# A fused adaLN block with sliding attention and MLP: V of the last blocks four at a time, Q and K of the last tokens two head groups at a time, and a new order of the work

## The chip, the cores and the metric

The kernel runs on one core of one Trainium2 chip. The metric is the device time of one execution in microseconds (us). The engines are TensorE (PE; its weight loads are PEld), VectorE (DVE), ScalarE (ACT), GpSimd (POOL) and SyncE (SP), which here only issues DMAs.

## The reference

One sequence of 2048 tokens, width 448, 16 heads of 28, all in bf16. A vector `c` gives six modulation vectors. The attention looks back at 8 tokens at distance 2, so each token sees only tokens of its own parity.

```python
mod = (_silu(c) @ w_mod).reshape(c.shape[0], 6, 1, -1)      # sa, ca, ga, sb, cb, gb
h = _layernorm(x, axis=-1) * (1 + ca) + sa
x = x + ga * _A_ref(h, A_wqkv, A_wo)    # q, k, v = h @ wqkv; W, dil = (8, 2); softmax; @ wo
h = _layernorm(x, axis=-1) * (1 + cb) + sb
x = x + gb * _B_ref(h, B_w1, B_b1, B_w2, B_b2)   # layernorm, gelu(y @ w1 + b1) @ w2 + b2
```

## The kernel before, in words

Tokens are split by parity, so that the window becomes 8 neighbours. The 2048 tokens are 16 blocks of 128; everything stays in SBUF, apart from V, which goes through a DRAM buffer `vd` and comes back in another layout (`vb`).

**The steps**, each an item of a plan in `build_plan`, with the names that the text below uses:

- Front: loads; c's column; the first modulation column (`mcol`); filler matmuls on zeros (28 of them, L469) that keep TensorE busy while it has no work.
- First norm of each pair of blocks: statistics (`st`, L532), power on GpSimd (L539), normalised z (L550). z is transposed on TensorE for blocks 0 to 7 (L566) and by a DMA transpose for blocks 8 to 15 (L558), then modulated (`md`, L598 on ScalarE, L601 on VectorE) into `hT`.
- Q and K of five chunks of tokens, 256, 256, 512, 512 and 512 (L626 for full matmuls, L633 for half ones), by groups of four heads: Q and K of one group in one item for the 512-token chunks, of two groups for the 256-token ones. Each output is copied from PSUM to `qT` or `kT` by ScalarE (L299) or VectorE (L301).
- V of a pair of blocks in an item (`v0` to `v7`, L626 and L633), copied to `hm` (L299, L301) and stored to `vd` (L700).
- Attention in nine groups of 4 x 57 tokens ("group" below, 0 to 8): logits (L733), four exponentials (L743), two mask multiplies on VectorE (L750), denominators (L777) and PV (L790) on TensorE, logarithm and exponential for the reciprocal (L800, L805), the multiply into `qT` (L814). V comes back by L766.
- Output projection of a block (L831), residual (L840), second and third norm (L858 to L889, and L852 for `xp`), DMA transposes of Y (L897).
- W1 of a quarter of 512 tokens in pairs of 128 hidden columns (also L626, L633), Gelu (L924), W2 of a block in two half blocks of seven matmuls (L940; the last block L947), the final add (L957), stores.
- The second modulation row for ga, sb, cb, gb: matmuls of L979, a copy (L990), four broadcast matmuls (L997), copies.

**K = 448** is three and a half times 128. `pair_mm` makes two outputs with three full matmuls each, and the two remaining halves lie on the upper and lower 64 rows of TensorE and run side by side. An item is fulls then halves, or halves then fulls (`flip`), as fits its neighbour.

**The order** is not written out. `Plan.schedule` makes it by simulating the engines on the host, with a cost for each item, a priority for each kind (`CFG["bias"]`), a slope by position in the sequence, and an offset for single items (`CFG["delta"]`, several hundred numbers). It also picks ScalarE or VectorE for items that may run on either, and the slot of each pool: 8 PSUM banks, 3 `hm`, 3 `et`, 3 `vb` and so on. The instructions are then issued in that order, each engine in its own queue, and wait on one another by semaphores. The work goes in phases: attention groups 0 to 4, quarter 0 of W1 and W2, attention groups 5 to 8, quarters 1 to 3.

Of the kernel before, what the change touches and what calls it, by code (L numbers as in the profile page):

```python
# [40 lines left out]
    "gq": 1,  # L41
# [27 lines left out]
class Plan:  # L69
# [6 lines left out]
    def val(self, pool, name=""):  # L76
        return Val(pool, name)
# [154 lines left out]
CFG["tail"], CFG["slope"], CFG["window"] = 0.1858, 17.1995, 0.0  # L232
CFG["bias"] = {
    "bce": (546.38, 4.897),
    "cst": (75.94, 0.657),
    "dn": (399.55, 0.542),
    "exp": (-406.64, 0.035),
    "gelu": (309.0, 40.0),
    "h2": (334.66, 18.223),
    "ln": (396.58, 5.539),  # L240
    "lt": (204.59, 1.826),
    "md": (-259.64, 17.242),
    "mk": (396.22, 0.921),
    "mod2": (-141.6, 4.226),
    "nm1": (-536.02, 0.758),
    "nm2": (350.15, 0.058),
    "on": (508.41, 0.329),
    "out": (-32.32, 40.0),
    "pow1": (425.38, 9.787),
    "pow2": (316.33, 35.34),  # L250
    "pv": (-105.38, 0.033),
    "qk": (-559.98, 40.0),
    "qke": (-451.84, 0.062),
    "rc": (-553.09, 1.822),
    "st1": (22.72, 6.097),
    "st2": (436.0, 12.774),
    "store": (505.92, 1.122),
    "v": (74.06, 0.479),
    "ve": (-464.55, 0.417),
    "vl": (119.35, 18.269),  # L260
    "vt": (-382.37, 0.418),
    "w1": (-470.64, 2.563),
    "w2": (-9.18, 7.592),
    "w2s": (-587.27, 3.145),
    "wcp": (241.56, 0.151),
    "wo": (592.51, 5.659),
    "wos": (184.89, 0.061),
    "x1": (-109.63, 0.131),
    "xp": (28.83, 0.137),
    "yt": (495.74, 0.753),  # L270
    "zt": (-447.45, 0.124),
    "ztp": (106.15, 15.848),
# [6 lines left out]
CFG['hold'] = 0.2  # L279
CFG['margin'] = 19.0  # L280
CFG['pen'] = {'bce': -0.36, 'front': -0.23, 'md': 0.11, 'mod2': 0.17, 'qke': 0.2, 've': -0.13, 'wcp': 1.87}
CFG['wlag'] = 2


class Names:
# [3 lines left out]
def build_plan(cfg):  # L289
# [64 lines left out]
    def fn(e):  # L354
        memset(e, T.nhalf[:], -0.5)
# [318 lines left out]


    vraw = val("hm", "vraw")

    def fn(e):
        for r0 in (0, 16 + S):
            T.nc.sync.dma_start(out=T.vd[r0:r0 + 16, :], in_=T.zero[0:16, 0:D])  # L680
    add("vdz", "vt", {"SP": 1.0}, fn, rd=["zero"], wr=["vdz"], land=(1.0, 32 * 896))
    for p in range(NB // 2):
        P.pos = 2.0 * p
        vs = [val("ps", f"v{p}{i}") for i in range(2)]

        def fn(e, p=p, vs=vs):
# [492 lines left out]
```

## Time and profile before

| | |
|---|---|
| median of 3 runs | 172.96 us (172.14 to 175.27) |
| profiled execution | 173.88 us |
| its span in the trace | 172.1 us |
| instructions | 5181 |

The profile is of one execution. A row of the timeline is start, duration, engine, line, operation, what it writes and reads, shapes, count, and in brackets the idle time before it and what ended that. Neighbouring instructions of one kind are one row; durations of matmuls are modelled and overlap, so that costs are read from one row's start to the next one's. Some matmul records are missing. "ps" is a PSUM bank.

### The profile page before, as it was taken

The numbers are of one execution on the slowest core, as the hardware profiler recorded it, in microseconds if no ns is written. First come the engines' busy times: TensorE is split into PE (matmuls) and PEld (weight loads), VectorE is DVE, ScalarE is ACT, GpSimd is POOL, SyncE is SP. The second block draws the span as 40 slices with busy tenths as digits, with TensorE's granted clock in tenths as the row PEclk, the third lists the DMA queues.
The fourth block names the chain that finished last, engine by engine and source line by source line (L and its number), as shares of the span: only waits on it lengthen the run. The fifth ranks groups of instructions, "written<-read, shape, count | busy, mean of one in ns | idle before, by whom it ended". The sixth has DMA issues, their size and how long they took to land.

```text
span 172.1 us, 5181 instructions
## 1 busy us (share of the span) xinstructions
PE 164.5 (96%) x2146; PEld 81.6 (47%) x2163; DVE 118.2 (69%) x325; ACT 108.5 (63%) x202; POOL 38.8 (23%) x63
## 2 busy tenths in 40 slices
PE   7999899999889999999999999999999999999993
PEld 2556355445435444344556454445433544355562
DVE  3679799998599999998458999998991110004121
ACT  3878995795897488969969793960057606840000
POOL 7213110422322311111052121314221040003000
PEclk9999999999999999999999999999999999999999
DMA  5999769575889994230312030033301130000311
GB/s 162 364 366 259 243 198 179 153 156 97 259 236 273 166 318 61 57 61 0 34 34 57 4 114 0 0 65 63 61 0 38 23 110 0 0 0 0 110 53 53
DMA packets 28622, 19.06 MB, mean 111 GB/s; under 512 B 14229, under 2 KB 28598, under 8 KB 28598
## 3 DMA queue, kind: packets, MB, share of 16 engines
q1 hardware_dynamic: 28182, 18.27, 41.3%
q10 hardware_dynamic: 416, 0.46, 0.9%
q8 instruction: 17, 0.28, 0.7%
q14 instruction: 7, 0.06, 0.1%
HBM read 11.87 MB, written 3.70 MB: 90 GB/s over the span
## 4 chain that ended last, share of the span: by engine, by line
PE 77%; DMA 13%; DVE 4%; SPq 2%; issue 1%; DVEq 0%
PE ps L626 33%; PE ps L940 23%; PE ps L831 7%; PE ps L633 6%; DMA hm<-in_w_mod_dram 6%; DMA x_all<-in_A_x_dram 3%; DMA hT<-z 3%; PE ps L790 2%; PE ps L733 2%; PE ps L947 2%; DMA vb<-vd 1%; DVE et L750 1%; PE ps L777 1%; DVE st L858 1%; SPq L436 1%
## 5 line engine op out<-in xcount | busy, mean ns | idle before, releaser
L924 ACT ACTIVATE hm<-ps,b1c 128x512 bf16<-128x512 f32 x56 | 33.8, 690 | 25.8 <-PE ps L633 23.9
L940 PE MATMUL ps<-w,hm 128*128 128x448 bf16 x210 | 41.4, 353 | 0.0
L626 PE MATMUL ps<-hT,w 128*128 128x512 bf16 x161 | 37.9, 379 | 0.5 <-issue 0.2
L957 DVE TENSOR_TENSOR x_all<-ps,xp 128x448 bf16<-128x448 f32 (+2 forms) x17 | 10.1, 595 | 33.8 <-PE ps L940 30.9
L940 PEld LDWEIGHTS <-hm 128*128 128x128 bf16 x210 | 20.1, 98 | 19.2 <-issue 0.6
L852 POOL TENSOR_TENSOR xp<-x_all,gbb 128x448 f32<-128x448 bf16 x16 | 17.0, 1063 | 45.8 <-DVE x_all L957 33.9
L626 PEld LDWEIGHTS <-w 128*128 128x128 bf16 x168 | 15.8, 98 | 20.7 <-issue 3.0
L866 POOL TENSOR_TENSOR rs<-tv,nhalf 128x2 f32<-128x2 f32 x16 | 12.0, 747 | 50.7 <-DVE tv L861 50.7
L626 PE MATMUL ps<-hT,Wqk 128*128 128x512 bf16 (+1 forms) x113 | 22.3, 335 | 0.7 <-issue 0.5
L743 ACT ACTIVATE et<-ps 128x464 bf16<-128x464 f32 x36 | 17.4, 576 | 5.3 <-PE ps L733 5.1
L626 PEld LDWEIGHTS <-Wqk 128*128 128x128 bf16 x120 | 10.7, 98 | 9.2 <-issue 2.4
L831 PE MATMUL ps<-wo,qT 128*128 128x448 bf16 x64 | 14.1, 354 | 0.7 <-DVE qT L814 0.7
L750 DVE TENSOR_TENSOR et<-et,mask 128x928 bf16<-128x928 bf16 x18 | 10.9, 633 | 4.3 <-ACT et L743 4.1
L539 POOL TENSOR_TENSOR rs<-tv,nhalf 128x2 f32<-128x2 f32 x8 | 6.3, 784 | 23.4 <-DVE tv L535 14.1
L814 DVE TENSOR_TENSOR qT<-ps,rec 128x456 bf16<-128x456 f32 x18 | 10.7, 626 | 1.0 <-ACT rec L805 0.8
L299 ACT CAST qT<-ps 128x512 bf16<-128x512 f32 x15 | 8.9, 595 | 3.4 <-PE ps L633 3.4
L299 ACT CAST kT<-ps 128x512 bf16<-128x512 f32 x15 | 8.9, 596 | 2.7 <-PE ps L633 1.9
L626 PE MATMUL ps<-Wv,hT 128*128 128x448 bf16 x48 | 10.4, 354 | 0.0
L532 DVE BATCH_NORM_STATS2 st<-x_all 128x6 f32<-128x448 bf16 x16 | 9.2, 614 | 1.9 <-DMA x_all<-in_A_x_dram 1.9
L840 DVE TENSOR_TENSOR x_all<-ps,x_all 128x448 bf16<-128x448 f32 x16 | 9.7, 619 | 0.7 <-PE ps L831 0.3
L805 ACT ACTIVATE rec<-rec 128x464 f32<-128x464 f32 x18 | 9.9, 594 | 0.1
L800 ACT ACTIVATE rec<-ps 128x464 f32<-128x464 f32 x18 | 9.2, 574 | 0.9 <-PE ps L777 0.9
(93 smaller groups left out, 194.2 us busy)
## 6 DMA issues: line engine op xcount, KB each, us to landing
w<-in_B_w_dram SPq DMA_DIRECT2D x6, 448.0 KB, 5.1
hm<-in_w_mod_dram SPq DMA_DIRECT2D x5, 448.0 KB, 5.6
vb<-vd SPq DMA_DIRECT2D x18, 112.0 KB, 3.2
vd<-hm SPq DMA_DIRECT2D x8, 224.0 KB, 4.5
x_all<-in_A_x_dram SPq DMA_DIRECT2D x3, 448.0 KB, 6.0
out_dram<-x_all SPq DMA_DIRECT2D x3, 448.0 KB, 3.5
hm<-in_A_wqkv_dram SPq DMA_DIRECT2D x2, 448.0 KB
w<-in_B_w_dram SPq DMA_DIRECT2D x2, 336.0 KB
```

Of the source, the lines that this page charges most:

```text
L299: T.nc.scalar.copy(out=out, in_=in_)
L626: nc.tensor.matmul(outs[o], lhsT=stat(o, sl, 0, 128), rhs=mov(o, sl, 0, 128), start=(i == 0 and not flip and o // 2 % nb == 0), stop=(i == ...
L633: nc.tensor.matmul(outs[o], lhsT=stat(o, sl, lo, lo + 64), rhs=mov(o, sl, lo, lo + 64), start=(flip and o // 2 % nb == 0), stop=(not flip ...
L743: T.nc.scalar.activation(out=T.et[ev.slot][:, r * 464:(r + 1) * 464], in_=psf(lv[r])[:, 0:464], func=ACT.Exp, scale=float(DH) ** -0.5)
L750: T.eng[e].tensor_tensor(out=t, in0=t, in1=T.mask[:], op=ALU.mult)
L814: T.nc.vector.tensor_tensor(out=T.q[:, :, c0:c0 + 2 * SQ], in0=v4(psf(po[u])[:, 0:464]), in1=v4(T.rec[rv.slot][:]), op=ALU.mult)
L831: T.nc.tensor.matmul(psf(vs[a])[:, 0:D], lhsT=T.q[:, m, c0:c0 + 128], rhs=T.wo[:, m, :], start=(m == 0), stop=(m == 3))
L852: T.eng[e].tensor_tensor(out=T.xp[xpv[b].slot][:], in0=T.x[:, b, :], in1=T.gbb2[:], op=ALU.add)
L866: T.nc.gpsimd.tensor_tensor(out=T.rs2[i][:, bs[0]:bs[0] + 2], in0=T.tv2[i][:, bs[0]:bs[0] + 2], in1=T.nhalf[:, 0:2], op=ALU.pow)
L924: T.nc.scalar.activation(out=T.hm[hmv[q].slot][:, 512 * f:512 * f + 512], in_=psf(v)[:, 0:512], func=ACT.Gelu_apprx_tanh, bias=T.b1c[:, f: ...
L940: T.nc.tensor.matmul(psf(v)[:, 0:D], lhsT=T.hm[hmv[q].slot][:, 512 * f + 128 * (b % 4):512 * f + 128 * (b % 4) + 128], rhs=T.w2[:, f, :], ...
L957: T.nc.vector.tensor_tensor(out=T.x[:, b, c0:c1], in0=psf(vs[i])[:, c0:c1], in1=T.xp[xpv[b].slot][:, c0:c1], op=ALU.add)
```

## The change

It does three things. V of blocks 8 to 15 is made in two items of four blocks (`v4`, `v6`; 14 matmuls' time and four banks each) in place of four items of two. Q and K of the last chunk (tokens 1536 to 2047) are made for two head groups in an item in place of one, so in two items of four outputs in place of four of two. And all numbers of the order are new: bias, delta, tail, slope, hold, margin and penalties. One load's latency in the plan's costs goes to 2.0; that changes no instruction by itself.

The diff, with the tables of numbers cut to a line or two:

```diff
-    "gq": 1,
+    "gqs": [2, 2, 1, 1, 2],
+    "vs": [1, 1, 1, 1, 2, 2],
...
-CFG["tail"], CFG["slope"], CFG["window"] = 0.1858, 17.1995, 0.0
+CFG["tail"], CFG["slope"], CFG["window"] = 0.0841, 10.9323, 0.0
...
-    "v": (74.06, 0.479),
+    "v": (-486.72, 5.423),
...
-CFG['hold'] = 0.2
-CFG['margin'] = 19.0
+CFG['hold'] = 0.17
+CFG['margin'] = 23.0
...
-            load(f"ldwmod2{hh}{j}", 256 * 896 * 2, fn, [("wmod2", hh, j)], vals=[wv], lag=3)
+            load(f"ldwmod2{hh}{j}", 256 * 896 * 2, fn, [("wmod2", hh, j)], vals=[wv], lag=3, lat=2.0)
...
-        g = cfg["gq"] if n == 512 else 2
+        g = cfg["gqs"][ci]
...
-    for p in range(NB // 2):
-        P.pos = 2.0 * p
-        vs = [val("ps", f"v{p}{i}") for i in range(2)]
+    p0 = 0
+    for gv in cfg["vs"]:
+        P.pos = 2.0 * p0
+        nv = 2 * gv
+        vs = [val("ps", f"v{p0}{i}") for i in range(nv)]
...
-        add(f"v{p}", "v" if p else "front", {"PE": 7 * MM[448] + 0.05}, fn,
-            rd=[("h", sl, b) for sl in range(4) for b in (2 * p, 2 * p + 1)] + [("Wv", 0), ("Wv", 1)],
-            wr=[("psv", p)], vals=vs, mode=("f", "h"))
+        add(f"v{p0}", "v" if p0 else "front", {"PE": 7 * gv * MM[448] + 0.05}, fn,
+            rd=[("h", sl, b) for sl in range(4) for b in range(2 * p0, 2 * p0 + nv)] + [("Wv", 0), ("Wv", 1)],
+            wr=[("psv", p0 + i) for i in range(gv)], vals=vs, mode=("f", "h"))
```

On TensorE the order of the items from the first V to the first W1 was, with "lt", "dn" and "pv" for logits, denominators and PV of a group, "qk2.1" for chunk 2 and head group 1, "zt" for a block's transpose on TensorE, "m2" and "bcm" for the modulation row and its broadcast, "wo" for a block's projection, and * for halves first:

```
before: v0 qk0.0* qk0.2 b1t zt2 zt3 lt0 zt4 zt5 v1 zt6 m2 zt7 dn0 qk1.0 v2* bcm v3 pv0 qk1.2 qk2.2* wo0 lt1 qk2.0
  qk2.3* dn1 pv1 qk2.1 v4* wo1 wo2 lt2 v5 lt3 qk3.2 dn2 pv2 qk3.0 qk3.1* wo3 dn3 pv3 wo4 v6 v7* wo5 wo6 qk3.3
  qk4.0* lt4 qk4.2 qk4.3* qk4.1 dn4 pv4 w10.6
after: v0 qk0.0* qk0.2 b1t zt3 zt2 lt0 zt4 zt5 v1 qk1.2* dn0 m2 zt7 zt6 pv0 v2 qk1.0* bcm v3 lt1 qk2.3 qk2.0* wo0
  dn1 pv1 qk2.1 qk2.2* wo1 wo2 lt2 qk3.2 lt3 qk3.3 dn2 pv2 qk3.1 v4* wo3 wo4 dn3 pv3 qk3.0 v6* wo5 wo6 lt4 qk4.0
  qk4.2* dn4 pv4 w10.6
```

In the phase after it, logits of groups 6, 7, 5 and 8 stand after 0, 3, 4 and 6 half blocks of W2 (before: 5, 6, 7, 8 after 1, 4, 6 and 7), and the projections of blocks 12 to 15 have moved ahead of the quarter's second pair of W1 items.

VectorE around the masks of group 2 (`et_86`) before; L601 is a modulation of four blocks that were transposed by DMA, L875 and L878 are the second norm of the first two blocks:

```order
L861 TENSOR_SCALAR tv_137<-mv_135 128x2
L840 TENSOR_TENSOR x_all<-ps_69,x_all 128x448
L601 TENSOR_SCALAR hT<-hT,mcol 128x512
L750 TENSOR_TENSOR et_86<-et_86,mask 128x928 x2
L875 TENSOR_SCALAR z_104<-x_all,mv_135,rs_139 128x448
```

And in the changed kernel, with the masks of group 3 (`et_84`) and the two modulations further on:

```order
L868 TENSOR_SCALAR tv_137<-mv_135 128x2
L847 TENSOR_TENSOR x_all<-ps_65,x_all 128x448
L757 TENSOR_TENSOR et_86<-et_86,mask 128x928 x2
L882 TENSOR_SCALAR z_104<-x_all,mv_135,rs_139 128x448
...
L757 TENSOR_TENSOR et_84<-et_84,mask 128x928
L821 TENSOR_TENSOR qT<-ps_65,rec_90 128x4x114
L896 TENSOR_SCALAR y_100<-z_104,mv_136,rs_140 128x512
...
L604 TENSOR_SCALAR hT<-hT,mcol 128x512
L821 TENSOR_TENSOR qT<-ps_71,rec_91 128x4x114
```

The modulation stood ahead of group 2's masks and now stands behind group 3's.

VectorE in the front before, around the copy of b1's column (`b1c`), which reads a small transpose on TensorE:

```order
L550 TENSOR_SCALAR z_96<-x_all,mv,rs 128x512
L550 TENSOR_SCALAR z_97<-x_all,mv,rs 128x512
L532 BN_STATS st<-x_all 128x6 x2
L534 BN_AGGR mv<-st 128x2 x2
L535 TENSOR_SCALAR tv<-mv 128x2
L1027 CAST b1c<-ps_67 128x14
L550 TENSOR_SCALAR z_98<-x_all,mv,rs 128x512
```

The same place in the changed kernel:

```order
L553 TENSOR_SCALAR z_96<-x_all,mv,rs 128x512
L553 TENSOR_SCALAR z_97<-x_all,mv,rs 128x512
L1034 CAST b1c<-ps_67 128x14
L535 BN_STATS st<-x_all 128x6 x2
L537 BN_AGGR mv<-st 128x2 x2
L538 TENSOR_SCALAR tv<-mv 128x2
L553 TENSOR_SCALAR z_98<-x_all,mv,rs 128x512
```

The copy moved ahead of the third pair's statistics.

ScalarE around the exponentials of group 3 before (L743 into `et_84`, from four banks; L299 evicts, L800 is the logarithm of group 2's denominators):

```order
L743 ACTIVATE et_84<-ps_69 128x464
L743 ACTIVATE et_84<-ps_71 128x464
L743 ACTIVATE et_84<-ps_67 128x464
L743 ACTIVATE et_84<-ps_64 128x464
L800 ACTIVATE rec_91<-ps_70 128x464
L800 ACTIVATE rec_90<-ps_66 128x464
L299 CAST kT<-ps_68 128x512
```

In the changed kernel, where the bank of the last of them (`ps_69`) is the fourth that the four-block V item `v4` takes:

```order
L750 ACTIVATE et_84<-ps_65 128x464
L750 ACTIVATE et_84<-ps_71 128x464
L750 ACTIVATE et_84<-ps_70 128x464
L302 CAST qT<-ps_64 128x512
L807 ACTIVATE rec_90<-ps_68 128x464
L807 ACTIVATE rec_91<-ps_67 128x464
L302 CAST kT<-ps_66 128x512
L750 ACTIVATE et_84<-ps_69 128x464
```

The fourth exponential moved behind two evictions and both logarithms.

More of the change, by code (lines that the diff above doesn't have):

```diff
@@ L230, in schedule @@
         return order
-CFG["tail"], CFG["slope"], CFG["window"] = 0.1858, 17.1995, 0.0
+CFG["tail"], CFG["slope"], CFG["window"] = 0.0841, 10.9323, 0.0
 CFG["bias"] = {
[L234 to L257, printed above, removed]
-    "v": (74.06, 0.479),
[L259 to L272, printed above, removed]
@@ new lines @@
+    "bce": (349.2, 0.192),
+    "cst": (-381.14, 0.61),
+    "dn": (466.63, 7.055),
+    "exp": (99.13, 10.173),
+    "gelu": (352.47, 0.031),
+    "h2": (116.49, 30.095),
+    "ln": (322.63, 0.04),
+    "lt": (563.97, 0.071),
+    "md": (-413.83, 40.0),
+    "mk": (593.01, 0.043),
+    "mod2": (-134.27, 0.501),
+    "nm1": (-132.68, 0.049),
+    "nm2": (-32.1, 0.132),
+    "on": (111.51, 0.029),
+    "out": (-355.74, 1.609),
+    "pow1": (-167.42, 0.021),
+    "pow2": (153.06, 0.179),
+    "pv": (-564.18, 0.535),
@@ new lines @@
+    "qk": (-301.42, 37.046),
+    "qke": (-322.78, 0.026),
+    "rc": (-547.22, 7.66),
+    "st1": (30.32, 4.106),
+    "st2": (238.08, 19.025),
+    "store": (457.5, 40.0),
+    "v": (-486.72, 5.423),
+    "ve": (-216.83, 0.227),
+    "vl": (165.72, 0.035),
+    "vt": (-351.09, 1.259),
+    "w1": (-310.1, 11.301),
+    "w2": (-158.31, 40.0),
+    "w2s": (-596.38, 8.632),
+    "wcp": (585.64, 3.469),
+    "wo": (597.16, 0.805),
+    "wos": (-61.62, 2.224),
+    "x1": (219.66, 8.298),
+    "xp": (-219.11, 5.747),
@@ L273 @@
+    "yt": (190.22, 0.507),
+    "zt": (-599.56, 0.873),
+    "ztp": (23.32, 1.787),
 }
@@ L282 @@
+CFG['hold'] = 0.17
+CFG['margin'] = 23.0
+CFG['pen'] = {'bce': 0.66, 'front': -0.23, 'md': 0.08, 'mod2': -0.49, 've': 1.29, 'wcp': 0.64}
 CFG['wlag'] = 2
+CFG['gqs'] = [2, 2, 1, 1, 2]
+CFG['vs'] = [1, 1, 1, 1, 2, 2]
 class Names:
@@ L689, in fn @@
                     lambda o, sl, lo, hi: T.Wv[lo:hi, sl, :])
[L690 to L703 removed]
+        add(f"v{p0}", "v" if p0 else "front", {"PE": 7 * gv * MM[448] + 0.05}, fn,
+            rd=[("h", sl, b) for sl in range(4) for b in range(2 * p0, 2 * p0 + nv)] + [("Wv", 0), ("Wv", 1)],
+            wr=[("psv", p0 + i) for i in range(gv)], vals=vs, mode=("f", "h"))
+        for p in range(p0, p0 + gv):
+            for i in range(2):
+                def fn(e, b=2 * p + i, v=vs[2 * (p - p0) + i]):
+                    copy(e, T.hm[vraw.slot][:, D * b:D * b + D], psf(v)[:, 0:D])
+                add(f"ve{2 * p + i}", "ve", {"ACT": 0.46, "DVE": 0.58}, fn, rd=[("psv", p)], wr=[("vr", 2 * p + i)],
+                    vals=[vs[2 * (p - p0) + i], vraw])
+            def fn(e, p=p):
+                T.nc.sync.dma_start(out=T.vd[16 + 256 * p:16 + 256 * p + 256, :].rearrange("(i p) n -> p i n", p=128),
+                                    in_=T.hm[vraw.slot][:, 2 * D * p:2 * D * p + 2 * D].rearrange("p (i n) -> p i n", i=2))
+            add(f"vt{p}", "vt", {"SP": 0.5}, fn, rd=[("vr", 2 * p), ("vr", 2 * p + 1)], wr=[("vd", p)], vals=[vraw],
+                land=(1.8, 256 * 896 * 1.2))
+        p0 += gv
     phase_of = {}
```

15 lines of the change are left out of this document (2 added, 13 removed).

## The prediction, made before the result was known

> **What bounds the kernel now.** I read the page first, then the windows, then TensorE's timeline for every place where it sat idle, then VectorE's and ScalarE's timelines for what it had waited for.
>
> ```profile
> span 172.1 us, 5181 instructions
> PE 164.5 (96%) x2146; PEld 81.6 (47%) x2163; DVE 118.2 (69%) x325; ACT 108.5 (63%) x202; POOL 38.8 (23%) x63
> PEclk9999999999999999999999999999999999999999
> PE 77%; DMA 13%; DVE 4%; SPq 2%; issue 1%; DVEq 0%
> ```
>
> TensorE is busy for 164.5 of 172.1 us at the full granted clock, and most of the chain that ended last lies on it. What a change can win is therefore its idle time, its overheads between matmuls, and no more. The windows say where these are:
>
> ```profile
> 40.00:50.00 10.00, 9.26 (x242) 4.65 (x243) 7.83 (x21) 7.34 (x17) 2.74 (x3) 1.00 0.75 203
> 50.00:60.00 10.00, 9.25 (x123) 4.46 (x122) 9.95 (x25) 7.01 (x14) 3.88 (x4) 1.00 1.07 218
> 60.00:70.00 10.00, 9.79 (x184) 4.38 (x184) 9.66 (x29) 8.27 (x17) 1.46 (x2) 1.00 0.71 172
> 80.00:90.00 10.00, 10.00 (x249) 5.57 (x248) 5.39 (x13) 7.99 (x15) 3.02 (x3) 1.00 0.23 28
> ```
>
> The columns are the stretch, its length, then busy TensorE, weight loads, VectorE, ScalarE, GpSimd. TensorE lacks 0.75 us in each of the stretches from 40 to 60, where VectorE is nearly full (9.95 of 10), and nothing from 80 on. On its timeline these are all the idle times after 20 us that something released:
>
> ```profile
> 20.74 0.67 PE L979 MATMUL ps<-hm,silu_bc 128*32 128x448 bf16 x6 [0.52 <-DMA hm<-in_w_mod_dram]
> 46.39 0.28 PE L777 MATMUL ps<-et,one 64*32 64x232 bf16 x4 [0.36 <-DVE et L750]
> 46.94 0.38 PE L777 MATMUL ps<-et,one 64*32 64x232 bf16 x12 [0.27 <-DVE et L750]
> 51.88 0.93 PE L831 MATMUL ps<-wo,qT 128*128 128x448 bf16 x4 [0.70 <-DVE qT L814]
> ```
>
> That is 0.52 us for the modulation weights, and 0.36 + 0.27 + 0.70 = 1.33 us for VectorE. Idle time put down to "issue" (0.16 us, beside a run of five matmuls out of six) is a missing record.
>
> **Term A, fewer changes of matmul shape.** Each item of Q/K, V or W1 is a run of full matmuls (F, 128 rows) and a run of half ones (H, two of 64 rows side by side); the order alternates F-H and H-F, so that neighbours share a run.
>
> ```profile
> 54.53 1.30 PE L626 MATMUL ps<-Wv,hT 128*128 128x448 bf16 x6
> 55.76 0.55 PE L633 MATMUL ps<-Wv,hT 64*128 64x448 bf16 x4
> 56.24 1.31 PE L626 MATMUL ps<-Wv,hT 128*128 128x448 bf16 x6
> 57.39 1.68 PE L831 MATMUL ps<-wo,qT 128*128 128x448 bf16 x8
> ...
> 74.30 2.75 PE L626 MATMUL ps<-hT,w 128*128 128x512 bf16 x12
> 76.98 1.04 PE L633 MATMUL ps<-hT,w 64*128 64x512 bf16 x8
> 77.95 2.76 PE L626 MATMUL ps<-hT,w 128*128 128x512 bf16 x11
> ...
> 150.49 16.05 PE L940 MATMUL ps<-w,hm 128*128 128x448 bf16 x84
> 166.38 2.85 PE L947 MATMUL ps<-w,hm 128*128 128x288 bf16 x28
> ```
>
> From start to start, 84 matmuls of 448 columns took 15.89 us, 0.189 each. Six in a row with the same shape behind them took 1.15 (56.24 to 57.39), six with halves behind them 1.23 (54.53 to 55.76), and four halves, two and two, 0.48 where 2 x 0.189 = 0.38 would do. So a change of shape costs 0.10 us. The eight halves of 512 columns say the same (0.97 against 4 x 0.217).
> Counted over the order, TensorE's shape runs fall from 89 to 79. Ten changes at 0.10 are -1.0 us; no matmul is added or removed. The low end is -0.4, if those among them that stand in stretches paced by VectorE or the front buy nothing. I take -1.0, since the trace has TensorE idle for so little.
> The Trainium skill's TensorEngine Tiling (Array Packing), Key Properties, says that a change of tiling mode drains TensorE; the 0.10 us agrees that there is a price. TensorE: Matmul & The Clock Gate, Single matmul latency, puts the warm constant of one matmul at 398 cycles of 2.4 GHz, 0.166 us; as an estimate, ten full drains by that page are -1.7 and the sum below 0.7 lower. The measured 0.10 decides.
>
> **Term B, the waits on VectorE.** The 0.36 and 0.27 come from this:
>
> ```profile
> 45.37 0.41 DVE L601 TENSOR_SCALAR hT<-hT,mcol 128x512 bf16<-128x512 bf16 x1 [1.96 <-DMA hT<-z]
> 45.70 1.19 DVE L750 TENSOR_TENSOR et<-et,mask 128x928 bf16<-128x928 bf16 x2
> ```
>
> VectorE stood 1.96 us before a modulation of blocks 12 to 15, waiting for their transposes, with group 2's masks queued behind it. In the new order those masks come straight after the residual add, and the modulations after group 2's second normalising multiply or on ScalarE. The 0.70 is the output projection of block 3 waiting for group 2's multiply, late by the same 2 us; between the two TensorE now has a V item of four blocks. I take -1.3; the ends are -1.33 and 0, since VectorE has little slack there. Late next is the first Y (two norms behind the masks), which nothing needs before W1 at 68 us.
>
> **Term C, the front.**
>
> ```profile
> 9.82 0.65 DVE L301 COPY Wqk<-hm 128x448 bf16<-128x448 bf16 x3 [1.57 <-DMA hm<-in_A_wqkv_dram]
> 14.03 1.14 DVE L532 BATCH_NORM_STATS2 st<-x_all 128x6 f32<-128x448 bf16 x2
> 14.49 0.18 PE L1023 MATMUL ps<-ident,b1r 14*128 14x14 bf16 x1
> 17.19 0.59 PE L469 MATMUL ps<-zero 128*128 128x512 bf16 x2
> 17.62 1.30 PE L626 MATMUL ps<-Wv,hT 128*128 128x448 bf16 x6
> 21.99 1.48 PE L626 MATMUL ps<-hT,Wqk 128*128 128x256 bf16 x12
> 23.41 0.39 PE L633 MATMUL ps<-hT,Wqk 64*128 64x256 bf16 x4
> ```
>
> Before, three fillers (two recorded at 17.19) and the 0.52 us wait stood before the modulation rows. Now a Q/K item of 1.42 + 0.3 us is done there: up to 0.52 + 3 x 0.217 = 1.2 us won. Against it: the copy of b1's column now stands ahead of the third statistics. It needs the tiny transpose at 14.49, so VectorE, free at 14.03 (plus 0.65 / 3 = 0.2 for a fourth weight copy), waits to about 14.9. Its later work is some 0.7 us late: 0.2 at the transposes of blocks 4 and 5, 0.2 at the first denominators. The broadcast matmuls take four banks at once, one of which ScalarE frees late in a row of ten operations (0.35), and one more filler precedes the first V (0.15). Net -0.3; the ends are -1.2 (no loss) and +0.9 (no gain).
>
> **Term D, new waits.**
>
> ```profile
> 35.97 0.69 DVE L301 CAST kT<-ps 128x512 bf16<-128x512 f32 x1
> 42.19 1.91 ACT L743 ACTIVATE et<-ps 128x464 bf16<-128x464 f32 x4 [2.07 <-PE ps L733]
> 56.17 1.96 ACT L299 CAST hm<-ps 128x448 bf16<-128x448 f32 x4 [0.87 <-PE ps L633]
> 60.72 0.58 ACT L299 CAST qT<-ps 128x512 bf16<-128x512 f32 x1 [2.60 <-PE ps L633]
> 82.61 1.28 ACT L1146 ACT_TABLE_LOAD   x1
> 83.91 1.91 ACT L743 ACTIVATE et<-ps 128x464 bf16<-128x464 f32 x4
> 87.44 1.91 ACT L743 ACTIVATE et<-ps 128x464 bf16<-128x464 f32 x4 [1.63 <-PE ps L733]
> ```
>
> One operation of ScalarE takes 0.48 us of its queue. The four-block V item begins with halves and so needs four banks at once; the fourth is freed by group 3's last exponential, now behind an eviction, two logarithms and another eviction: 5 x 0.48 = 2.4 us, while TensorE has 2.0 to 2.3 us of denominators, PV and Q/K. I put 0.4 there. In the second attention stage three groups of logits now follow one another by 2 to 3 half blocks of W2 (0.189 x 7 = 1.32 each), while four exponentials take 1.91: 0.35 in all. For places that I didn't follow I add 0.45. Together +1.2; the ends are 0, as before from 53 us on, and four full evictions (4 x 1.9 = 7.6), far from a trace that shows ScalarE waiting 2.07 and 2.60 us for TensorE.
>
> At nothing: VectorE gets five more Q/K evictions (two before, seven now; 0.6 of its time each, the row at 35.97) and one weight copy, and gives up one V eviction, two modulation copies and two modulations of 0.33: some +0.7 us, hidden by the 1.96 that goes. SyncE's queue: transposes 10 and 11 now stand behind a V store that waits for two evictions, the modulation that needs them is a microsecond later still; all four W1 loads leave before the first Y transpose, which waits longer than they do; group 7's V loads stand behind four Y transposes and group 6's PV, with four projections and half blocks as cover. The last stage issues the same matmuls; one W2 block more follows the last W1.
>
> Sum: -1.0 - 1.3 - 0.3 + 1.2 = -1.4 us. Against the profiled execution's 173.88 that is 172.5. The runs' median, 172.96, stands 0.92 below that execution, so I predict 171.6.
>
> **Rivals.** *Eviction binds (slower).* Two V and two Q/K items now claim four of the eight banks each. If each waits for the four evictions of its banks' last holder (1.9 us, the row at 56.17), D is 4 x 1.9 = 7.6, and 172.96 - 2.6 + 7.6 = 178.0; it decides from 1.5 us an item (-2.6 + 6.0 is 2% slower). For it speaks that the banks are claimed at once; against it the ScalarE waits above. The Trainium skill's Trainium Kernel Development and Optimization, Best Practices, warns of just this: tiling speeds TensorE but not the emptying of PSUM. By that rule the rival holds; the trace so far doesn't bear it out.
> *VectorE paces the attention stage (no gain).* It is busy 9.95 and 9.66 of 10 from 50 to 70 us. If it sets the pace, A, B and C are lost and its 0.7 us more shows: 172.96 + 0.7 = 173.7. Against it: TensorE waited for it 1.33 us only, and it waited 1.96 itself.
> *No new waits (faster).* The whole front is won and D is 0: -1.0 - 1.3 - 1.2 = -3.5, 169.4. For it: the old order had almost no waits from 53 us on.
>
> **How the numbers follow.** Two per cent, about what a measurement of this kernel can tell from no change, is 3.5 us: 169.5 and 176.4. Forecast 0.61 (170.0 to 173.0); VectorE paces 0.15; both within 2%, so 0.76 for the same. No new waits 0.12: faster. Eviction binds, or a stage that I didn't follow, 0.12: slower. The range leaves out the far eviction cases and little below: 169.2 to 174.6.
>
> **What would show it.** The first W1 now:
>
> ```profile
> 68.79 1.46 PE L626 MATMUL ps<-hT,w 128*128 128x512 bf16 x5
> ```
>
> One of its six is missing, so it starts at 68.6; with A to C in it and little of D it should start 1.5 to 2 us earlier. A: the second V item of four reads as 12 F after one H run, its neighbours' step near 2.7 us. B: no idle before the denominators (L777's successor) and no 2 us wait of VectorE. C: a Q/K item before the modulation rows; the wait of 0.52 gone. D: idle of TensorE, released by ScalarE, before the V halves and among the later groups' logits. Wrong would be idle of several us in one stage, or a first W1 that is no earlier.

## The result and the profile after

The changed kernel takes 171.6 us (median of 19 runs, 170.92 to 172.37); the kernel before, run beside it, 173.3 us (19 runs, 172.14 to 175.27). The ratio is 0.9898, with a 95% interval of 0.9877 to 0.992: about 1.75 us less, which is no change by the two per cent of a single measurement, but a real gain over so many runs. The profiled execution took 171.89 us with a span of 170.2, against 173.88 and 172.1.

The page of the changed kernel, the line of its span, the one of the engines' busy time, and the shares of the chain by engine:

```profile
span 170.2 us, 5183 instructions
PE 164.2 (96%) x2146; PEld 82.1 (48%) x2163; DVE 119.5 (70%) x326; ACT 107.4 (63%) x201; POOL 39.5 (23%) x63
PE 77%; DVE 9%; DMA 5%; ACT 4%; issue 2%; POOL 1%; SPq 1%; DVEq 0%
```

TensorE is still the bound: 164.2 us of work in a span that is 1.9 us shorter. Its idle time shrank by more than its work. The windows over the four stretches shown before the change, with the same columns:

```profile
40.00:50.00 10.00, 9.82 (x240) 5.03 (x218) 9.83 (x26) 9.30 (x20) 4.10 (x4) 1.00 0.78 211
50.00:60.00 10.00, 9.82 (x187) 4.93 (x187) 9.93 (x28) 7.38 (x16) 3.45 (x4) 1.00 0.92 223
60.00:70.00 10.00, 9.90 (x127) 4.33 (x127) 9.59 (x25) 7.21 (x14) 1.01 (x1) 1.00 0.55 148
80.00:90.00 10.00, 10.00 (x263) 5.45 (x261) 6.34 (x15) 9.52 (x19) 3.52 (x3) 1.00 0.17 35
```

From 40 to 60 us TensorE now lacks 0.18 us a stretch where it lacked 0.75, and VectorE, which stood 1.96 us there, is as full from 40 to 50 as from 50 to 60 (9.83 and 9.93). Doing so much without TensorE waiting, it was not what paced this stage. TensorE's timeline, all rows from 20 us on with a wait that an engine or a load released (three rows in all, where there were four before):

```profile
32.93 0.93 PE L838 MATMUL ps<-wo,qT 128*128 128x448 bf16 x4 [0.18 <-DVE wo L1019]
34.03 0.39 PE L784 MATMUL ps<-et,one 64*32 64x232 bf16 x16 [0.17 <-DVE et L757]
95.96 3.96 PE L838 MATMUL ps<-wo,qT 128*128 128x448 bf16 x20 [0.15 <-DVE qT L821]
```

The four waits of before (0.52, 0.36, 0.27, 0.70) are gone; the three new ones add up to 0.50 by the brackets. But a bracket counts only from the modelled end of the row ahead, and read from one start to the next these places cost more. From the full matmuls at 31.28 to the output projection at 32.93 are 1.65 us, where the same step takes 1.31 elsewhere (36.86 to 38.17); from that projection to the denominators are 1.10, against 0.85 (91.97 to 92.82); from the half block of W2 at 94.31 to the projections at 95.96 are 1.65, against 1.33 (90.64 to 91.97). So the three cost 0.34, 0.25 and 0.32 us. A fourth place has no bracket: the eight matmuls of two projections from 49.88 to 51.73 take 1.85 us instead of 1.60 (57.02 to 58.62), because the second projection waits, as the row of its weight loads shows:

```profile
50.87 0.49 PEld L838 LDWEIGHTS <-qT 128*128 128x128 bf16 x4 [0.51 <-DVE qT L821]
```

By starts the waits of before were larger too: 1.75 us for VectorE instead of 1.33 (45.64 to 46.39 where 0.32 would do, 46.39 to 47.06 for 0.21, 49.71 to 51.88 for 1.31), and 0.89 for the modulation weights instead of 0.52 (the 16 matmuls took 1.87 from 19.47 to 21.34, and take 0.98 after the change). The places that the prediction named, on the same timeline:

```profile
19.25 0.38 PE L636 MATMUL ps<-hT,Wqk 64*128 64x256 bf16 x4
19.56 1.48 PE L629 MATMUL ps<-hT,Wqk 128*128 128x256 bf16 x12
...
21.54 1.05 PE L986 MATMUL ps<-hm,silu_bc 128*32 128x448 bf16 x16
...
47.09 0.58 PE L636 MATMUL ps<-Wv,hT 64*128 64x448 bf16 x4
47.60 2.44 PE L629 MATMUL ps<-Wv,hT 128*128 128x448 bf16 x12
49.88 1.93 PE L838 MATMUL ps<-wo,qT 128*128 128x448 bf16 x8
...
66.69 1.46 PE L629 MATMUL ps<-hT,w 128*128 128x512 bf16 x5
```

The Q/K item fills the place ahead of the modulation rows, which run in one piece. The four-block V item takes 49.88 - 47.09 = 2.79 us with no wait on its fourth bank. The first W1 starts at 66.69 instead of 68.79, so 2.10 us earlier, a little more than the 1.5 to 2 that was forecast. (The prediction took 0.2 us off before's row for a record that is missing; a later profile of the changed kernel has all six records in a row of the same 1.46 us, so the missing one lies inside, and starts are read as the rows give them. Where an expectation below says 66.47, the row's 66.69 is meant.) The end came 1.94 us earlier. So the whole gain is there by the first W1, and nothing is added behind it.

VectorE's timeline of the changed kernel, six places:

```profile
15.24 0.17 DVE L1034 CAST b1c<-ps 128x14 f32<-128x14 bf16 x1 [0.96 <-PE ps L1030]
...
29.45 0.63 DVE L1015 TENSOR_TENSOR gbb<-gb,b 128x448 f32<-128x448 bf16 x1 [1.26 <-DMA b<-in_B_b_dram]
...
31.57 1.30 DVE L1019 TENSOR_TENSOR wo<-wo,ga 128x448 bf16<-128x448 bf16 x4
32.79 1.18 DVE L757 TENSOR_TENSOR et<-et,mask 128x928 bf16<-128x928 bf16 x2
...
42.19 2.04 DVE L757 TENSOR_TENSOR et<-et,mask 128x928 bf16<-128x928 bf16 x2
...
49.87 0.40 DVE L604 TENSOR_SCALAR hT<-hT,mcol 128x512 bf16<-128x512 bf16 x1
50.19 0.62 DVE L821 TENSOR_TENSOR qT<-ps,rec 128x456 bf16<-128x456 f32 x1
```

The masks of group 2 at 42.19 come with no wait for a transpose ahead of them: that is term B. The copy of b1's column waits 0.96 us for its small transpose, much as the prediction said (it put 0.7). What it did not see is the product for the gates (L1015), which waits 1.26 us for the load of b2: the scaling of the output weights and the masks of group 1 stand behind it, and they are what TensorE waits for at 32.93 and 34.03. The last two rows are the fourth place: a modulation at 49.87 stands ahead of the second half of group 2's multiply, which ends at 50.81, and the second projection starts behind it.

### The profile page after: what moved, and what is told of

The parts are those of the page before. It is cut to its first block, busy times and chain, and to the rows that moved or that the text cites. A ratio compares the mean times of both kernels' runs of the same rounds, so it can differ in the third digit from the quotient of the medians.

```text
span 170.2 us, 5183 instructions
## 1 busy us (share of the span) xinstructions
PE 164.2 (96%) x2146; PEld 82.1 (48%) x2163; DVE 119.5 (70%) x326; ACT 107.4 (63%) x201; POOL 39.5 (23%) x63
## 4 chain that ended last, share of the span: by engine, by line
PE 77%; DVE 9%; DMA 5%; ACT 4%; issue 2%; POOL 1%; SPq 1%; DVEq 0%
PE ps L629 31%; PE ps L947 22%; PE ps L838 6%; PE ps L636 6%; PE ps L472 4%; DVE et L757 4%; DMA b<-in_B_b_dram 3%; PE ps L740 2%; ACT et L750 2%; PE ps L797 2%; PE ps L954 2%; DMA hT<-z 2%; PE ps L784 1%; ACT hT L601 1%; DVE qT L821 1%
## 5 line engine op out<-in xcount | busy, mean ns | idle before, releaser
L859 POOL TENSOR_TENSOR xp<-x_all,gbb 128x448 f32<-128x448 bf16 x16 | 17.7, 1114 | 48.0 <-DVE x_all L964 34.9
L757 DVE TENSOR_TENSOR et<-et,mask 128x928 bf16<-128x928 bf16 x18 | 13.1, 744 | 3.4 <-ACT et L750 3.3
L838 PE MATMUL ps<-wo,qT 128*128 128x448 bf16 x64 | 13.6, 353 | 0.4 <-DVE wo L1019 0.2
L302 ACT CAST kT<-ps 128x512 bf16<-128x512 f32 x13 | 8.2, 629 | 3.3 <-PE ps L629 3.0
L472 PE MATMUL ps<-zero 128*128 128x512 bf16 x25 | 8.6, 483 | 1.5 <-DVE oz L307 1.3
L838 PEld LDWEIGHTS <-qT 128*128 128x128 bf16 x64 | 5.9, 98 | 7.3 <-DVE qT L821 1.4
```

Source lines behind the costliest of these rows:

```text
L472: T.nc.tensor.matmul(psf(fvl)[:, 0:512], lhsT=T.zero[:, 0:128], rhs=T.zero[:], start=True, stop=True)
L757: T.eng[e].tensor_tensor(out=t, in0=t, in1=T.mask[:], op=ALU.mult)
L838: T.nc.tensor.matmul(psf(vs[a])[:, 0:D], lhsT=T.q[:, m, c0:c0 + 128], rhs=T.wo[:, m, :], start=(m == 0), stop=(m == 3))
L859: T.eng[e].tensor_tensor(out=T.xp[xpv[b].slot][:], in0=T.x[:, b, :], in1=T.gbb2[:], op=ALU.add)
```

## The experiments

The theory was the prediction's: fewer shape changes (A), a modulation that no longer holds up VectorE (B), and a filled front (C), less some new waits (D). The rivals were that a shape change costs more or nothing, that B and C are covered anyway, and that the larger items bring the gain by themselves. Each ratio is to the kernel before, run beside that kernel on the same chip. The moves are made in the finished order, behind the scheduler.

### Shape changes put back, eight and thirty-two

At the start of `pair_mm`, an item of four outputs is issued as two runs of two:

```
+        if nb == 1 and len(outs) == 4 and T.it.name in ('v4', 'v6', 'qk4.0', 'qk4.2'):
+            for a in (0, 2):
+                pair_mm(outs[a:a + 2], lambda o, sl, lo, hi, a=a: stat(o + a, sl, lo, hi),
+                        lambda o, sl, lo, hi, a=a: mov(o + a, sl, lo, hi))
+            return
```

> The changed kernel in the same order, but each of its four new items (two of V, two of Q and K) issues its matmuls as two sub-items of two outputs, halves and fulls in turn, so that TensorE's shape changes go up by 8 (79 runs to 87) and nothing else moves. If a change of shape costs 0.10 us and TensorE paces this stage: +0.8 us, 172.4 beside 171.6, the four items longer by about 0.2 us each in the trace. If VectorE paces the stage and the grouping buys nothing: +0.0 to +0.2. If each change were a full drain of 0.166 us: +1.3.

Measured: 172.38 us (12 runs), ratio 0.9946, 0.9917 to 0.9975. That is 0.0048 of 173.3 over the changed kernel's ratio, 0.83 us for eight changes, or 0.10 each; the two intervals just touch, so the trace has to carry it. TensorE's timeline of this kernel, the V item and the start and end of the Q/K items:

```profile
46.95 0.35 PE L641 MATMUL ps<-Wv,hT 64*128 64x448 bf16 x2
47.23 1.31 PE L634 MATMUL ps<-Wv,hT 128*128 128x448 bf16 x6
48.47 0.36 PE L641 MATMUL ps<-Wv,hT 64*128 64x448 bf16 x2
48.77 1.31 PE L634 MATMUL ps<-Wv,hT 128*128 128x448 bf16 x6
49.92 0.54 PE L843 MATMUL ps<-wo,qT 128*128 128x448 bf16 x2
...
59.26 1.47 PE L634 MATMUL ps<-hT,Wqk 128*128 128x512 bf16 x5
...
66.05 0.39 PE L789 MATMUL ps<-et,one 64*32 64x232 bf16 x16
```

The same 16 matmuls of V take 49.92 - 46.95 = 2.97 us in four runs, where two runs took 2.79: two changes, 0.09 each. The Q/K items take 66.05 - 59.26 = 6.79 us; in the changed kernel they stand from 59.26 to the denominators at 65.62, 6.36: four changes, 0.11 each.

> The same split for all sixteen items of four outputs, the twelve of W1 too: 32 shape changes more than the changed kernel. At 0.10 us each +3.2 us, 174.8; at 0.166 us each +5.3, 176.9; if only the W1 quarters are paced by TensorE +2.4, 174.0.

All 16 items of four outputs were split (the condition on the names is dropped), 32 changes more. Measured: 175.44 us (4 runs), ratio 1.0106, 1.005 to 1.0162; 3.84 over the changed kernel's median, 3.6 by the ratios. Its trace has the wait for b2's load too, longer (1.77 us on VectorE), and TensorE waits 0.69 + 0.17 us behind it, 0.51 more than in the changed kernel. (3.84 - 0.51) / 32 = 0.10 again, and the same from 3.6. So A is linear, at 0.10 us a change. At the 0.166 us that the prediction took from the Trainium skill (TensorE: Matmul & The Clock Gate, Single matmul latency), 32 changes would have been 5.3 us.

### The modulation alone, moved late in the kernel before and early in the changed one

In the kernel before (`md12.2` is VectorE's modulation of blocks 12 to 15, `y0` the first Y):

```
+order.remove(by['md12.2'])
+order.insert(order.index(by['y0']) + 1, by['md12.2'])
```

> The kernel before with one item moved: the modulation of blocks 12 to 15 that stood ahead of group 2's masks on VectorE now stands behind the first Y, as in the changed kernel. If the waits on VectorE were this one item's doing: the idle of 0.36, 0.27 and 0.70 us before the denominators and the projection of block 3 goes, -1.3 us, 172.0 beside 173.3. If VectorE paces the stage and its other work takes the place: 0.0 to -0.3.

Measured: 173.05 us (12 runs, 172.12 to 173.59), ratio 0.9973, 0.9943 to 1.0003: between 0 and 1 us won, where 1.3 was at stake. TensorE's timeline of this kernel:

```profile
50.82 0.93 PE L831 MATMUL ps<-wo,qT 128*128 128x448 bf16 x4 [0.38 <-ACT rec L805]
...
67.68 1.46 PE L626 MATMUL ps<-hT,w 128*128 128x512 bf16 x5
```

The waits before the denominators are gone. The output projection of block 3 still waits, 0.38 us, now for ScalarE's reciprocal (L805) instead of VectorE's multiply. The first W1 comes 1.11 us earlier (68.79 to 67.68), but the span ends only 0.5 earlier (171.6), so about half was given back behind W1. (Its front happened to start 0.65 us later, with the first V at 9.27 instead of 8.62; from the first V to the first W1 it is 1.76 us shorter, 0.4 of that because the modulation weights came earlier.) Behind W1 the trace shows one place, a gap of 0.43 us in the middle of a PV item at 99.3 us for which no releaser is recorded; whether it is in every execution is not known. So the experiment confirms where the waits came from; the time of the whole kernel doesn't confirm the size.

In the changed kernel, back to where it stood, behind block 2's residual add (`x12`):

```
+order.remove(by['md12.2'])
+order.insert(order.index(by['x12']) + 1, by['md12.2'])
```

> The kernel after with one move: VectorE's modulation of blocks 12 to 15 goes back to right behind block 2's residual add, ahead of group 2's masks, as before the change. Work and shape runs are the same. Theory (term B: that place costs TensorE about 1.2 us of waits): VectorE stands 1.5 to 2 us there again, TensorE waits before group 2's denominators and before the output projection of block 3 for 0.5 to 1.3 us, the first W1 starts 0.5 to 1.2 us later than 66.47, and the time rises by 0.5 to 1.2 us over the kernel after (ratio to before 0.993 to 0.997). Rival (the four-block V item now stands between, and covers the late masks, so that the change would have gained this without the move): first W1 within 0.2 us of 66.47, the ratio 0.989 to 0.991.

Measured: 173.38 us (12 runs), ratio 0.9993, 0.9965 to 1.002, apart from the changed kernel's interval: 1.6 us, the whole gain, lost by one instruction's place. VectorE's timeline there:

```profile
43.34 0.41 DVE L604 TENSOR_SCALAR hT<-hT,mcol 128x512 bf16<-128x512 bf16 x1 [2.05 <-DMA hT<-z]
43.67 1.19 DVE L757 TENSOR_TENSOR et<-et,mask 128x928 bf16<-128x928 bf16 x2
```

And TensorE's, three rows:

```profile
44.91 0.39 PE L784 MATMUL ps<-et,one 64*32 64x232 bf16 x16 [0.82 <-ACT qT L302]
...
51.51 0.93 PE L838 MATMUL ps<-wo,qT 128*128 128x448 bf16 x4 [0.39 <-DVE qT L821]
...
67.36 1.46 PE L629 MATMUL ps<-hT,w 128*128 128x512 bf16 x5
```

VectorE stands 2.05 us for the transposes with the masks behind it, as before the change, and TensorE waits 0.82 + 0.39 = 1.21 us by the brackets, before group 2's denominators and before the second of the two projections behind the V item. By starts these are 0.88 and 0.55, and the changed kernel itself has 0.25 at the second place. (The first is put down to ScalarE, whose eviction came last by the profile; the masks end at 44.86, just before the denominators start at 44.91, so it is the masks.) This execution did not have the wait for b2's load. Counted from group 1's denominators (33.48 here, 34.03 in the changed kernel) to the first W1, it loses 33.88 - 32.66 = 1.22 us, which is what 0.88 + 0.55 - 0.25 comes to. The rival, that the V item between them would have covered the late masks, falls: it covers the first of the two projections and no more.

### The Q/K item in the front put back

On TensorE, behind the modulation rows (`m2`):

```
+order.remove(by['qk1.2'])
+order.insert(order.index(by['m2']) + 1, by['qk1.2'])
```

> The kernel after with one move: the Q/K item of chunk 1 that stands ahead of the modulation rows (20 matmuls, 1.42 us) goes behind them, so that TensorE has nothing between the 128-column Q/K items before and the modulation rows. Theory (term C: that item covers a wait for the modulation weights and the time until the next work is ready): TensorE waits about 1 us before the modulation rows, and the first W1 and the end come 0.7 to 1.4 us later (ratio to before 0.994 to 0.998). Rival (a later wait of the front is only moved, as group 0's masks or the transposed blocks pace it): the time rises by under 0.3 us, ratio 0.989 to 0.991.

Measured: 173.17 us (12 runs), ratio 0.999, 0.9956 to 1.0024: 1.6 us lost, again about the whole gain. TensorE's timeline:

```profile
20.68 0.28 PE L784 MATMUL ps<-et,one 64*32 64x232 bf16 x4 [0.97 <-DVE et L763]
21.52 0.38 PE L784 MATMUL ps<-et,one 64*32 64x232 bf16 x12 [0.57 <-DVE et L763]
...
67.87 1.46 PE L629 MATMUL ps<-hT,w 128*128 128x512 bf16 x5
```

TensorE waits 1.54 us, for group 0's masks and not for the modulation weights: the item had covered VectorE's work. The first W1 is 1.18 us later, although this execution lacked the waits for b2's load. The place to be filled was 1.5 us wide where the prediction counted 1.2.

### The waits left in the front

The product for the gates (`gbb2`) goes behind group 1's masks in three kernels, and in two of them b1's copy goes behind the third statistics too:

```
+order.remove(by['gbb2'])
+order.insert(order.index(by['mk1.0']) + 1, by['gbb2'])

+order.remove(by['b1c'])
+order.insert(order.index(by['st3']) + 1, by['b1c'])
```

> The changed kernel with the product of gb and b2 moved behind group 1's masks on VectorE. In the trace of the changed kernel VectorE stood 1.26 us before it, waiting for b2's load, and TensorE then waited 0.18 and 0.17 us for what is queued behind it. If those two waits are the product's doing: they go, -0.35 us, 171.25. If the stage is full anyway, 0.0, with the waits moved elsewhere.

Measured: 171.02 us (6 runs), ratio 0.9868, 0.9828 to 0.9907, some 0.5 us under the changed kernel, with overlapping intervals. VectorE's timeline, with the product behind these two and no wait for b2 any more:

```profile
29.61 1.30 DVE L1019 TENSOR_TENSOR wo<-wo,ga 128x448 bf16<-128x448 bf16 x4
31.10 1.19 DVE L757 TENSOR_TENSOR et<-et,mask 128x928 bf16<-128x928 bf16 x2 [0.20 <-ACT et L750]
```

The output weights are scaled at 29.61 instead of 31.57 and TensorE's 0.18 and 0.17 are gone; the first W1 starts at 65.75, 0.94 earlier. Of that, 0.23 is a front that started earlier by itself (the first V at 8.86 instead of 9.09). The other 0.71 is mostly the two waits, which cost 0.34 + 0.25 = 0.59 us by starts: here the projection comes 1.31 us after the full matmuls (31.20 to 32.51) and the denominators 0.85 after it.

> The kernel after, word for word, once more, as the base for the two runs beside it on the same chip. Its trace also tells whether the 1.26 us that VectorE stood for b2's load (and TensorE's waits of 0.18 and 0.17 behind it) is in every execution: the profiles with the same order up to there have it in one (1.77 us, the run with all items of four split) and not in three. Theory (the load lands at another time in each execution): ratio to before 0.988 to 0.992 whether the wait is there or not.

Measured: 171.64 us (6 runs, 171.10 to 171.98), ratio 0.9889, 0.9844 to 0.9933: the changed kernel again. VectorE's product stands 1.23 us in this execution too, and TensorE waits 0.17 at the denominators. (The profile puts the product's wait down to ScalarE, but b2's load was issued at 24.41 and landed 5.3 us later, just ahead of the product at 29.82. In the first experiment the same load, issued at 24.39, had landed by 28.49, where the product started without a wait.) Of the seven profiles with nearly the same order up to that place, four have the wait (1.26, 1.77 and 1.23 us, and 1.48 in the last kernel below) and three have none. So it depends on when the load lands in the execution.

> The kernel after with the two moves on VectorE alone, all fillers kept: the product for the gates that needs b2's load goes behind group 1's first masks, b1's column copy behind the third statistics. Theory (C's loss: the copy's wait of 0.96 us delays the later transposes and group 0's masks; the fillers left out in the run before brought a wait of 0.72 us for a copied weight and so no gain): group 0's masks come 0.3 to 0.7 us earlier on VectorE, the end 0.2 to 0.5 us earlier than after, ratio 0.986 to 0.989. Rival (the front is set by loads and TensorE's own work, VectorE's wait is covered): within 0.2 us of the kernel after beside it, ratio 0.988 to 0.992.

Measured: 170.96 us (6 runs, 170.67 to 171.63), ratio 0.986, 0.9816 to 0.9904: the fastest of all, 0.7 under the changed kernel beside it, though the intervals of the ratios overlap, and no better than the first move alone (0.9868). VectorE's timeline shows why the second move brings nothing:

```profile
18.98 0.64 DVE L757 TENSOR_TENSOR et<-et,mask 128x928 bf16<-128x928 bf16 x1 [0.92 <-ACT et L750]
```

Without the wait for the copy, VectorE gets to group 0's masks earlier and there waits 0.92 us for ScalarE's exponentials; with the copy ahead, in the kernel of the first move alone, it waited 0.32 at the same place. With the first move alone the masks start at 19.11, 0.13 later, and so does the first V (8.86 instead of 8.73), so nothing is won. The loss that C charged for the copy was covered.

> The kernel after with two moves on VectorE and three fillers of TensorE left out: the product for the gates that waited 1.26 us for b2's load goes behind group 1's first masks, b1's column copy goes behind the third statistics, and three of the 512-column fillers ahead of the first V are dropped (the fillers compute nothing). Theory: both moves take waits of VectorE away that stood ahead of work TensorE needs; 0.4 to 0.6 us for the first move (0.35 of it the two waits of TensorE that it causes), 0.1 to 0.3 for the second and up to 0.4 for the fillers, where the first V was ready before they ended: ratio to before 0.982 to 0.988. Rival (the first V waits for its transposed blocks anyway, and VectorE's 0.96 us is covered): no better than the first move alone, ratio 0.986 to 0.988.

This kernel has both moves, and leaves out three fillers besides (`fill18`, `fill21`, `fill22`). Measured: 171.75 us (8 runs), ratio 0.9922, 0.989 to 0.9954: no better than the changed kernel. One row of TensorE's timeline, then one of VectorE's:

```profile
11.12 0.40 PE L636 MATMUL ps<-hT,Wqk 64*128 64x256 bf16 x4 [0.72 <-ACT Wqk L302]
```

```profile
33.56 0.41 DVE L604 TENSOR_SCALAR hT<-hT,mcol 128x512 bf16<-128x512 bf16 x1 [1.10 <-DMA hT<-z]
```

Where two fillers stood, TensorE waits 0.72 us for a copied weight. The first V does start earlier (8.27 instead of 9.09), and most of that is lost here. Later VectorE is early and waits 1.10 us for transposes that land when they land, and in the second attention stage TensorE waits 0.30 us for V and 0.43 with no releaser recorded. The fillers had covered the wait for the weight rather than caused one; the expectation on them was wrong.

### Items and order, each with the other's old half

```
 # new items, before's numbers and noise        # old items, the new numbers and noise
 CFG["gqs"] = [2, 2, 1, 1, 2]                   CFG["gqs"] = [2, 2, 1, 1, 1]
 CFG["vs"] = [1, 1, 1, 1, 2, 2]                 CFG["vs"] = [1, 1, 1, 1, 1, 1, 1, 1]
```

> The new items (V of blocks 8 to 15 in fours, Q and K of the last chunk in twos) with the kernel before's numbers and noise for the order: the larger items alone. Shape runs of TensorE end at 86 instead of before's 89, the modulation of blocks 12 to 15 stands ahead of group 2's masks as before, the front is the kernel before's. Theory (A by 0.10 us a change; B and C come from the order and not from the items): 0.3 us under the kernel before for the shapes, up to 0.4 lost or won at the four-bank items: ratio 0.996 to 1.001. Rival (larger items bring the gain themselves): ratio 0.989 to 0.993. Second rival (four banks claimed at once wait for evictions): over 1.003, with waits of TensorE for ScalarE at the four-bank items.

Measured: 174.32 us (6 runs), ratio 1.0093, 1.0056 to 1.013: slower than before, and both the theory and the first rival missed. TensorE's timeline:

```profile
48.77 0.38 PE L783 MATMUL ps<-et,one 64*32 64x232 bf16 x12 [0.35 <-DVE et L756]
...
52.20 0.54 PE L635 MATMUL ps<-Wv,hT 64*128 64x448 bf16 x4
...
68.67 0.74 PE L783 MATMUL ps<-et,one 64*32 64x232 bf16 x16 [0.76 <-DVE et L756]
70.24 1.46 PE L628 MATMUL ps<-hT,w 128*128 128x512 bf16 x5 [0.26 <-ACT rec L806]
```

The four-bank items do not wait here either, so the second rival is right about the time and wrong about the place. The waits are 0.35 + 0.76 us for masks, 0.26 before the first W1 for a bank that ScalarE's logarithm (L806) reads, 0.75 ahead of the modulation rows, as in the old front, and a gap of 0.76 in a PV item with no releaser recorded: 2.88 us, where the kernel before has 1.85 in all. The first W1 starts 1.45 us later than before; of the other 0.4 us, 0.33 is a front that started later by itself (the first V at 8.95 instead of 8.62). The larger items alone bring nothing; the planner lays the work out anew around them.

> The counterpart of the run with the new items in the old order: the new numbers and noise with the old items (V of blocks 8 to 15 in pairs, Q and K of the last chunk in single head groups). Shape runs of TensorE end at 83 (89 before, 79 after), but the planner also lays out the Q/K work of the last chunk otherwise than after. Theory (most of the gain lies in the order, since the larger items in the old order gave none): A is 6 x 0.10 = 0.6 us instead of 1.0, B and C are kept as far as the order is the same up to the last chunk: ratio to before 0.990 to 0.995. Rival (the order was chosen for the larger items and loses elsewhere without them): ratio 0.997 to 1.01, with new waits of TensorE after 50 us.

Measured: 178.28 us (6 runs), ratio 1.0264, 1.021 to 1.0317: 4.7 us slower, far beyond the rival's 1.01. The cause lies at 96 us, where denominators and PV of the last groups stand with no W1 or W2 between them. The windows of two us each (the last columns are the granted clock, the share of DMA and GB/s), and the row of TensorE's timeline behind them:

```profile
96.00:98.00 2.00, 0.84 (x87) 0.73 (x87) 1.19 (x2) 2.00 (x5) 0.00 (x0) 0.92 0.69 229
98.00:100.00 2.00, 0.71 (x65) 0.55 (x42) 1.40 (x3) 0.69 (x3) 0.00 (x0) 0.50 0.04 13
100.00:102.00 2.00, 2.00 (x6) 0.76 (x5) 1.92 (x4) 1.38 (x3) 0.00 (x0) 0.50 0.00 0
102.00:104.00 2.00, 2.00 (x7) 0.84 (x6) 0.64 (x2) 0.00 (x0) 1.04 (x1) 0.50 0.01 4
104.00:106.00 2.00, 2.00 (x11) 1.00 (x10) 1.27 (x3) 0.00 (x0) 0.00 (x0) 0.88 0.00 0
```

```profile
99.83 6.99 PE L838 MATMUL ps<-wo,qT 128*128 128x448 bf16 x24 [1.28 <-DVE qT L821]
```

TensorE is idle for 2.45 of the 4 us from 96 on. In the middle of them the granted clock falls to half: a mean of 0.92 from 96 to 98 puts the fall at about 97.7 us, and 0.88 from 104 to 106 puts its end at about 104.5, so it lasts nearly 7 us. 24 projection matmuls take 6.99 us in it, 0.29 each, where the changed kernel's 20 take 3.96 (the row at 95.96), 0.20 each. So some 2.2 us go to the clock, beside the idle time itself. This comparison says that the order was made for these items; it does not price them.

## Why the prediction was right

The time was predicted as 171.6, and 171.6 was measured. That the two are equal is luck: the forecast was 1.4 us off a median of 172.96, and measured were 1.7 off 173.3. The forecast of a small gain was right, and so were A and B; C and D came near in sum more than in their parts. Waits are read from start to start here, as in the section on the result.

**A, -1.0.** Right in price: 0.10 us a change, by eight and by thirty-two changes put back. Seven of the ten stand before the first W1 and are part of the 2.10 us won there. (By the shapes on the two timelines it is nine, six of them before the first W1.) The last three, worth 0.3, don't show: from the first W1 to the end the lead went from 2.10 to 1.94 us. That is 0.46 to be explained, of which the wait at 95.96 is 0.32; the rest, about 0.14 us, is not traced to a place. The Trainium skill's TensorEngine Tiling (Array Packing), Key Properties, says that a change of tiling mode drains TensorE; the runs agree that a change has a price.

**B, -1.3.** Right in place, and near in size: the three waits for VectorE are gone, worth 1.33 by the brackets and 1.75 by starts, and putting the modulation back costs 1.22 us up to the first W1 and 1.6 us of time. Taken alone in the kernel before, it won only 0.5 (0 to 1). "Late next" was right in kind and wrong in place: not the first Y, but a reciprocal on ScalarE there, and in the changed kernel the second half of group 2's multiply, behind a modulation.

**C, -0.3.** Right in sign, too small. Up to the first logits of group 1 (TensorE's timeline, before at 31.71, after at 28.70), the kernel before had done one Q/K item of 512 columns more (7 x 0.217 + 0.10 = 1.62) and one projection (0.85), so it stood at 29.24 for equal work: 0.54 won. But this execution's first V came 0.47 later (9.09 instead of 8.62, where 0.15 was charged), and that start differs between executions of one front: 8.62 to 9.27 in three profiles with the old one, 8.73 to 9.47 in nine with the new. From the first V on, 1.01 us were won. The place filled was 1.5 us wide instead of 1.2, the copy of b1's column cost nothing since the masks wait for ScalarE anyway, and the broadcast matmuls show no wait for a bank (0.35 was charged).

**D, +1.2.** Right in sum by luck, since its places were wrong. "I put 0.4 there", at the fourth bank of the V item, and nothing came: with a change at 0.10, the item would take 14 x 0.189 + 0.10 = 2.75 us and takes 2.79. The count was right (the bank comes free after 2.3 us of ScalarE's work), but TensorE's own work up to that bank was as long. ScalarE's rows in the changed kernel:

```profile
43.41 1.53 ACT L750 ACTIVATE et<-ps 128x464 bf16<-128x464 f32 x3
...
46.55 0.72 ACT L750 ACTIVATE et<-ps 128x464 bf16<-128x464 f32 x1
```

The last exponential ends at 47.27, just when the second pair of halves needs its bank. In the second attention stage the wait at 95.96 is 0.32 for the 0.35 forecast, but TensorE waits there for VectorE's multiply, and not among the logits for ScalarE's exponentials. The 0.45 "for places that I didn't follow" was 0.84: 0.59 in the two waits behind b2's load, which lands late only in some executions, and 0.25 at the second projection. In sum 1.16 for 1.2.

By stretches, the two profiled executions differ so: the first V comes 0.47 us later, from there to group 1's logits 1.01 are won, from these logits to the first W1 1.56, and behind it 0.16 are lost: -1.94 in all. The 1.56 are B's 1.75, some shape changes of A and small waits of before, less D's 0.84 and some smaller waits.

**The rivals.** *Eviction binds* falls: none of the four-bank items waits, in the changed kernel or in the one with the old numbers. The warning of the Trainium skill (Trainium Kernel Development and Optimization, Best Practices), that tiling speeds TensorE but not the emptying of PSUM, is not borne out at these four places. *VectorE paces* falls with the windows: it is full for 20 us while TensorE misses 0.36. But it was nearer than it looked, since one operation in the wrong place costs the whole gain. *No new waits* falls too: there are 1.16 us of them, and without the 0.59 behind b2's load, in the kernels with the product moved, the time was still 171.0 and not 169.4.

## What to carry to other kernels

Look at what an in-order engine does right before the work that the bound engine waits for: an operation that waits for a transfer, ahead of masks that are ready, cost TensorE 1.2 us or more for a modulation and some 0.6 for b2's product, and moving it behind them cost little. Read such waits from start to start: the brackets showed 0.50 us of new ones where 1.16 were lost. Whether a wait can be moved without loss shows on the next engine: the copy's 0.96 us and the fillers were covered, or covering something, and taking them away won nothing. Grouping halves and fulls of a matmul is worth its number of changes times 0.10 us, and no more; larger items in an order that wasn't laid out for them lost time.

## What the runs showed of the hardware that was not expected

- The granted clock of TensorE fell to half at about 97.7 us in the kernel with the old items, when TensorE had been idle for some 1.3 of the last 2.7 us, with no gap longer than 0.94. The gap of 1.28 us came after the fall. The clock rose again at about 104.5, after 4.7 us of busy time from 99.83 on. The Trainium skill's TensorE: Matmul & The Clock Gate, Part 1, gives an idle window of about 3.4 us as the condition of the fall; here shorter gaps were enough, as in another kernel that the same part tells of. The recovery after a few us of busy time agrees.
- The load of b2 landed late enough to hold VectorE for 1.2 to 1.8 us in four of seven executions with nearly the same order, and not at all in the others. It landed 5.3 to 5.5 us after its issue in three of the four, and in at most 4.1 us in the other three executions.
- A PV item shows gaps of 0.4 to 0.9 us in its middle with no releaser in the profile, in some executions (0.43, 0.76 and 0.94 us in three of the kernels here). What they wait for stays open.
